# A larger ring, streamed values and a finer schedule in a decode kernel that reads a key-value cache

## The chip, the cores and the metric

One core of one Trainium2 chip. The metric is device time in microseconds (us) of one execution. Every run named here was at a granted TensorE clock of 1.00. A run reads some 2 us longer than the span of its profile.

## The reference, cut to what matters

One token per row, eight rows. Two layers, each attention plus a feed-forward, both with the same weights and the same cache:

```python
x = x + attention(layernorm(x), k_cache, v_cache, wq, wo)   # 32 heads of 128, 4096 keys
x = x + relu(layernorm(x) @ w1) @ w2                         # 640 -> 1728 -> 640
x = x + attention(layernorm(x), k_cache, v_cache, wq, wo)   # the same cache again
x = x + relu(layernorm(x) @ w1) @ w2
```

In bf16 the cache is 8 x 32 x 4096 x 128 x 2 x 2 bytes = 537 MB, far more than the on-chip memory, and it is needed twice: 1074 MB, less what is still on the chip at the second reading. The weights are 15 MB.

## The kernel before

A *visit* is one row, one layer and one pair of heads. A *dip* is a stretch of lower transfer rate; there is one at every row's end. It needs 4 units of keys and 4 of values, each 512 KB (128 partitions x 4 KB). All units pass through one ring, the *arena*; TensorE frees a unit once it has read it, and only then can the next load into it be issued. Some units of a row (`keep`) stay until its second layer has used them. The order of all work is fixed on the host by `plan`:

```python
UNIT, G, SPARE, SMALL, AHEAD = 4, 22, 6, 4, 3      # units per visit half, units of ring, ...
    keep = set()                                   # G - SPARE = 16 units stay for layer 1
    ...
            roomy = G - len(kept)                  # how many units one load brings
            n = 4 if keeping or roomy >= 16 else 2 if roomy >= SMALL else 1
    ...
            visits += nxt[:AHEAD] + cur + nxt[AHEAD:]   # AHEAD visits of the next row, then layer 1
```

Between the units of a visit `step()` mixes in one piece of each waiting chain: softmax, output projection, and at a row's end the feed-forward (`up` and `down`, 70 matmuls each, in one piece) and 160 query matmuls in four pieces. The values, per visit 64 pairs of weight load and one-column matmul:

```python
    nc.tensor.matmul(oy[i][:, h : h + 1], lhsT=arena[:, value block], rhs=P_tiles[i][:, h, j : j + 1], ...)
```

## Time and profile before

| what | before |
|---|---|
| time, median of 4 runs | 2524.51 us (2523.44 to 2529.79) |
| bytes moved by all DMA queues | 1027.07 MB |
| TensorE busy | 55% |

### The profile page before, as it was taken

To read this page: it belongs to the slowest core of one execution; us is meant where nothing else is said; L and a number is where in the kernel's file an instruction comes from. 1 tells how busy PE (TensorE), PEld (TensorE's weight loads), DVE (VectorE), ACT (ScalarE), POOL (GpSimd) and SP (SyncE) were. 2 spreads that over 40 slices of the span, in tenths; PEclk is the share of its full clock that TensorE was granted. 3 is DMA by queue.
4 is the path that set the end of the run, shared out by engine and by line. 5 is a ranking of instruction groups with operands and counts; after the bars stand their busy time and mean duration, and the time that the engine had idled before them with its cause. 6 is when DMAs were issued, how large, how long until landed. Compare 5 with 4: busy or idle time off the path is not lost.

```text
span 2521.7 us, 84569 instructions
## 1 busy us (share of the span) xinstructions
PE 1384.2 (55%) x40134; PEld 1299.3 (52%) x40134; DVE 320.4 (13%) x1707; ACT 288.2 (11%) x1422; POOL 0.7 (0%) x6
## 2 busy tenths in 40 slices
PE   3447545475454754557455574545645466445745
PEld 3336545464454744546454564545645455444744
DVE  0001111111111111111111111111111111111111
ACT  1001001010010100101010110101101011001200
POOL 0000000000000000000000000000000000000000
DMA  9999999999999999999999999999999999999897
GB/s 408 424 426 377 419 425 426 423 345 426 425 425 422 360 426 425 425 406 372 425 426 425 400 386 426 425 426 386 403 425 425 426 375 413 426 425 404 324 427 305
DMA packets 82525, 1027.07 MB, mean 407 GB/s; under 512 B 9220, under 2 KB 9220, under 8 KB 9220
## 3 DMA queue, kind: packets, MB, share of 16 engines
q1 hardware_dynamic: 82180, 1021.68, 97.4%
q8 instruction: 313, 5.13, 0.8%
q14 instruction: 32, 0.26, 0.0%
HBM read 1021.63 MB, written 0.01 MB: 405 GB/s over the span
## 4 chain that ended last, share of the span: by engine, by line
DMA 76%; PE 19%; issue 3%; ACT 1%; SPq 0%; DVE 0%; ACTq 0%
DMA arena<-in_A_k_cache_dram 38%; DMA arena<-in_A_v_cache_dram 37%; PE s_ps L397 6%; PE oy_ps L399 6%; PE blk_ps L434 1%; PE q_ps L371 1%; DMA wq_sb<-in_A_wq_dram 1%; PE oy_ps L449 1%; PE ch_ps L321 1%; PE ch_ps L338 1%; PE blk_ps L410 1%; ACT L428 0%; PE blk_ps L419 0%; PE ch_ps L300 0%; ACT P_sb L428 0%
## 5 line engine op out<-in xcount | busy, mean ns | idle before, releaser
L397 PE MATMUL s_ps<-q,arena 128*128 128x1 bf16 x16384 | 517.8, 165 | 586.7 <-DMA arena<-in_A_k_cache_dram 535.7
L399 PE MATMUL oy_ps<-P_sb,arena 128*128 128x1 bf16 x16384 | 519.6, 166 | 509.8 <-DMA arena<-in_A_v_cache_dram 482.6
L397 PEld LDWEIGHTS <-arena 128*128 128x128 bf16 x16384 | 479.5, 104 | 608.2 <-DMA arena<-in_A_k_cache_dram 553.8
L399 PEld LDWEIGHTS <-arena 128*128 128x128 bf16 x16384 | 481.5, 105 | 555.6 <-DMA arena<-in_A_v_cache_dram 500.2
L423 ACT ACTIVATE nmax<-blk_ps 128x2 f32<-128x2 f32 x256 | 44.1, 172 | 1987.5 <-PE blk_ps L419 1987.5
L438 DVE RECIPROCAL invL<-blk_ps 128x2 f32<-128x2 f32 x256 | 43.8, 171 | 965.2 <-PE blk_ps L434 965.2
L414 DVE TENSOR_REDUCE hmx<-blk_ps 2x1 f32<-2x128 f32 x256 | 71.3, 279 | 734.5 <-PE blk_ps L410 734.5
L434 PE MATMUL blk_ps<-lrow,ones_c 128*128 128x2 f32 x512 | 145.2, 353 | 1.9 <-issue 1.9
L428 ACT ACTIVATE P_sb<-s_ps,nmax 128x32 bf16<-128x32 f32 x512 | 142.4, 283 | 7.8
L449 PEld LDWEIGHTS <-wo_sb 128*128 128x128 bf16 x2560 | 131.7, 121 | 9.5 <-issue 9.3
L434 PEld LDWEIGHTS blk_ps<-lrow,ones_c 128*128 128x128 f32 x512 | 128.7, 311 | 3.5 <-issue 2.0
L449 PE MATMUL oy_ps<-oT,wo_sb 128*128 128x1 bf16 x2560 | 104.9, 165 | 8.7 <-issue 8.4
L428 ACT ACTIVATION_READ_ACCUMULATOR P_sb<-s_ps,nmax 128x1 f32 x512 | 100.2, 196 | 0.0
L406 DVE TENSOR_REDUCE mrow<-s_ps 128x2 bf16<-128x64 f32 x256 | 57.5, 225 | 213.9 <-PE s_ps L397 213.9
L410 PE MATMUL blk_ps<-ident,mrow 128*2 128x128 bf16 x256 | 68.3, 267 | 4.4 <-issue 4.2
L442 DVE TENSOR_TENSOR oT<-oy_ps,invL 128x2 bf16<-128x2 f32 x256 | 40.8, 160 | 159.4 <-PE oy_ps L399 159.4
L371 PEld LDWEIGHTS <-wq_sb 128*128 128x128 bf16 x1440 | 43.2, 105 | 11.2 <-issue 7.9
L338 PEld LDWEIGHTS <-w_sb 128*128 128x128 bf16 x1120 | 45.3, 107 | 6.4 <-issue 4.4
L338 PE MATMUL ch_ps<-hT,w_sb 128*128 128x1 bf16 x1120 | 45.8, 168 | 4.0 <-issue 3.7
L456 DVE TENSOR_TENSOR xT<-xT,oy_ps 128x5 f32<-128x5 f32 x256 | 41.0, 160 | 46.4 <-PE oy_ps L449 25.2
L419 PE MATMUL blk_ps<-diag,onesb_c 2*128 2x2 bf16 x256 | 46.8, 183 | 0.0
L371 PE MATMUL q_ps<-xq,wq_sb 128*128 128x1 bf16 x1280 | 40.0, 165 | 7.4 <-issue 7.4
(42 smaller groups left out, 324.4 us busy)
## 6 DMA issues: line engine op xcount, KB each, us to landing
arena<-in_A_v_cache_dram SPq DMA_DIRECT2D x208, 2048.0 KB, 21.9
arena<-in_A_k_cache_dram SPq DMA_DIRECT2D x192, 2048.0 KB, 22.4
arena<-in_A_k_cache_dram SPq DMA_DIRECT2D x96, 1024.0 KB, 8.6
arena<-in_A_v_cache_dram SPq DMA_DIRECT2D x64, 1024.0 KB, 7.2
wq_sb<-in_A_wq_dram SPq DMA_DIRECT2D x4, 1280.0 KB, 25.0
wo_sb<-in_A_wo_dram SPq DMA_DIRECT2D x4, 1280.0 KB, 34.3
w_sb<-in_B_w_dram SPq DMA_DIRECT2D x1, 2240.0 KB, 36.6
w_sb<-in_B_w_dram SPq DMA_DIRECT2D x1, 2160.0 KB
```

What stands on the lines that cost most here:

```text
L338: nc.tensor.matmul(y_ps[:, c : c + 1], lhsT=w2_sb[:fs, f, c * P : (c + 1) * P], rhs=st[key, "hT"][:fs, f : f + 1], start=(f == 0), stop=(f ...
L371: nc.tensor.matmul(q_ps[:, h, :], lhsT=wq_sb[:, g, c, h * Dh : (h + 1) * Dh], rhs=xl[:, c : c + 1] if layer else xl[:, :, c], start=(c == ...
L397: nc.tensor.matmul(s_tiles[i][:, h, j : j + 1], lhsT=lhsT, rhs=q, start=True, stop=True)
L399: nc.tensor.matmul(oy[i][:, h : h + 1], lhsT=lhsT, rhs=P_tiles[i][:, h, j : j + 1], start=(j == 0), stop=(j == NJ - 1),)
L406: nc.vector.tensor_reduce(out=m_tiles[i], in_=s_tiles[i], axis=AX.X, op=ALU.max)
L410: nc.tensor.matmul(blk[i][:2, :P], lhsT=m_tiles.pop(i), rhs=ident, start=True, stop=True)
L414: nc.vector.tensor_reduce(out=hmx, in_=blk[i][:2, :P], axis=AX.X, op=ALU.max)
L419: nc.tensor.matmul(blk[i][:, P : P + 2], lhsT=ones_b, rhs=nmax.pop(i), start=True, stop=True)
L423: nc.scalar.activation(out=nm, in_=blk[i][:, P : P + 2], func=ACT.Copy, scale=-inv_sqrt_dh)
L428: nc.scalar.activation(out=P_tiles[i][:, h, :], in_=S[:, h, :], func=ACT.Exp, bias=nm[:, h : h + 1], scale=inv_sqrt_dh, accum_out=l_tiles[ ...
L434: nc.tensor.matmul(blk[i][:, P + 2 : P + 4], lhsT=ones_f, rhs=l_tiles.pop(i), start=True, stop=True)
L449: nc.tensor.matmul(oy[i][:, 2 + c : 3 + c], lhsT=wo_sb[:, 2 * hp + h, c * P : (c + 1) * P], rhs=o[:, h : h + 1], start=(h == 0), stop=(h = ...
```

## The change

The intent: read less, by keeping more of the cache; and let TensorE hold up the loads less in the stretch where the ring is squeezed. The core of the diff:

```diff
-G = 22      SPARE = 6    SMALL = 4    AHEAD = 3
+G = 26      SPARE = 6    SMALL = 7    AHEAD = 4    CAP = 20
     def step():
-        for c in chains:                       # one piece of every chain
+        n = 0                                  # cheapest first, at most CAP matmuls in one step
+        for c in sorted(chains, key=lambda c: c[0][0]):
+            if not n or n + c[0][0] <= CAP:
+                n += c[0][0]
+                take(c)
     # feed-forward and queries
-    up: 70 matmuls, down: 70 matmuls, queries: 4 pieces of 40
+    up: 5 pieces of up to 15, down: 5 pieces of 14, queries: 16 pieces of 10
     # values: the probabilities are the weights, the values stream
-    matmul(oy[:, h:h+1], lhsT=arena[value block], rhs=P_tiles[:, h, j:j+1])            # 64 per visit
+    matmul(o_ps[32*c : 32*c+CJ, :], lhsT=P_tiles[:, h, j:j+CJ], rhs=arena[512 columns],
+           tile_position=(0, 32*c))                                                     # 16 per visit
+    nc.scalar.copy(out=o_tiles, in_=o_ps)                                               # then 4 gathering matmuls
     # sum of the softmax: one bf16 matmul and a reduction instead of ACT's accumulator and an fp32 matmul
     # layer 1: output projection, norm and feed-forward once for all 8 rows at the end, not row by row
     # square root of the per-row norms: 12 VectorE instructions instead of ScalarE's Sqrt
-    nc = Bacc("TRN2", ...)
+    nc = Bacc("TRN2", ..., dynamic_dma_scratch_size=32)      # memory for the larger ring
     # (cuts marked by comments; the layout of V in memory changes with the value matmul)
```

## The prediction

> **What bounds the kernel now.** I read the page first (busy shares, the forty slices, the queues, the chain of waits), then the timeline in stretches of 20 us over the whole span, then the chain of waits and the groups by line inside one slow stretch.
>
> ```profile
> span 2521.7 us, 84569 instructions
> PE 1384.2 (55%) x40134; PEld 1299.3 (52%) x40134; DVE 320.4 (13%) x1707; ACT 288.2 (11%) x1422; POOL 0.7 (0%) x6
> ...
> GB/s 408 424 426 377 419 425 426 423 345 426 425 425 422 360 426 425 425 406 372 425 426 425 400 386 426 425 426 386 403 425 425 426 375 413 426 425 404 324 427 305
> DMA packets 82525, 1027.07 MB, mean 407 GB/s; under 512 B 9220, under 2 KB 9220, under 8 KB 9220
> ...
> q8 instruction: 313, 5.13, 0.8%
> ...
> DMA 76%; PE 19%; issue 3%; ACT 1%; SPq 0%; DVE 0%; ACTq 0%
> ```
>
> No compute engine is busy for more than 55% of the span, and DMA is 76% of the chain. The GB/s row shows a ceiling near 425, left only in eight short dips (once per batch row) and at the end. So the time is bytes over 425 GB/s, plus what the dips, head and tail lose. The stretches of 20 us show both states; columns are PE, weight load, DVE, ACT, POOL, PE clock, DMA share, GB/s.
>
> ```profile
> 440.00:460.00 20.00, 10.07 (x305) 9.45 (x303) 2.28 (x12) 1.64 (x10) 0.00 (x0) 1.00 1.01 425
> ...
> 500.00:520.00 20.00, 11.35 (x322) 10.48 (x319) 3.22 (x19) 2.92 (x11) 0.00 (x0) 1.00 0.88 341
> 520.00:540.00 20.00, 16.20 (x442) 15.49 (x443) 3.44 (x20) 6.30 (x18) 0.00 (x0) 1.00 0.95 335
> 540.00:560.00 20.00, 14.26 (x444) 13.45 (x442) 2.51 (x14) 2.14 (x13) 0.00 (x0) 1.00 0.97 367
> ...
> 2500.00:2520.00 20.00, 11.73 (x297) 10.83 (x297) 2.66 (x15) 2.60 (x9) 0.00 (x0) 1.00 0.20 84
> ```
>
> The 98 stretches at 415 GB/s or more average 425.2. For each of the others I take 20 x (1 - GB/s / 425.2): the first loses 2.7 us, the last 16.0, the eight dips 85.6 (8.1, 11.8, 9.7, 10.7, 9.4, 9.0, 8.8, 17.9). Check: 1027.07 MB / 425.2 GB/s = 2415.5, plus 104.3 = 2519.8, against a span of 2521.7. This balance carries the prediction.
>
> What a dip is: the second row of its chain of waits.
>
> ```profile
> 516.65 7.43 DMA arena<-in_A_v_cache_dram
> 524.13 1.01 PE oy_ps L399 x32
> 525.25 2.18 PE ch_ps L321 x70
> 527.43 0.95 PE s_ps L397 x32
> ...
> 528.81 2.67 PE ch_ps L338 x70
> ...
> 540.64 1.37 issue
> ```
>
> From 524 to 563 us the chain is nearly all PE and its "issue" gaps (1.4, 1.6, 2.2 us): the row's feed-forward in lumps of 70 matmuls, the 160 query matmuls, and visits whose keys and values are already resident, which cost PE time but no DMA. Before that (505 to 524) PE waits for 1 MB loads. The cause is the same: 16 of the ring's 22 units of 512 KB hold data for layer 1, so six feed the stream, in pieces of two units, and a unit is refilled only after PE has read it.
>
> **What the Trainium skill says.** "HBM Reference", section Access, gives about 425 GB/s for a core that streams alone, bounded by its 16 DMA engines; the 425.2 above agrees, so I treat it as a ceiling no schedule will lift. "DMA: Bandwidth & Descriptors", section Bandwidth, measured 341 GB/s for one 1 MB transfer alone and 425 for 16 MB. The dips' 335 to 367 resemble the first, but inside the same dip, when several 1 MB loads are queued, 406 to 439 appear in 2.5 us stretches: depth counts too. "SBUF — State Buffer", section SBUF size, gives 224 KiB per partition less 16 KiB of DMA scratch. Weights take 114.4 KiB and 22 units 88 KiB, 202.4 of 208; 26 units need 218.4, which is why the change cuts the scratch to 32 bytes. "TensorE: Matmul & The Clock Gate" (Back-to-back issue gap; Part 3) puts a warm 512-column matmul at N/2.4 + 2.5 ns, about 216 ns, and three concurrent column tiles at 2.38 times one. No instruction of this trace shows either; the clock column is 1.00 throughout.
>
> **The change, part by part.** I counted loads in the kernel's own static plan.
>
> Bytes. The ring grows to 26 units, 20 kept instead of 16, so each of 8 rows saves four more units: K/V traffic falls from 1006.6 to 989.9 MB, 16.8 MB or 39.5 us at 425.2. This is on the path: DMA is the bound.
>
> Instructions. PE's list shrinks from 79,352 rows to 52,866, so of 84.6 thousand instructions about 26 thousand go; 5.13 MB of fetch falls by about 1.6 MB, 3.7 us, and the issue gaps should be rarer.
>
> PE. Values: before, 64 matmuls and weight loads per visit (a 32-matmul half takes 1.01 us, so 2.0). After, the four columns of probabilities are stationary and the values stream, 16 matmuls of 512 columns in four column groups. Estimate from the skill: 16 x 216 ns = 3.45 us in series, 1.4 overlapped by 2.4. The softmax sum loses its two fp32 passes (0.56 us to about 0.2). The output projection (0.41 us) goes in seven of eight layer-1 rows, and seven layer-1 feed-forwards go (5 us each), done at the end for all rows at once. Added: four gathering matmuls, 0.15 us. In the steady state PE has half its time free, so none of this is on the path. In the dip it is: 2.0 + 1.4 + some 1.0 of small work per visit against 4.8 before.
>
> ACT and DVE. ACT gains one 100 x 512 copy per visit (estimate 0.56 us, from 165 ns at 2 columns and 213 at 64) and loses two accumulator reads (0.39) and its square-root table switches (two of 1.28 us each time); DVE gains about 12 instructions of 0.16 us per norm. Neither is over 20% busy; hidden.
>
> Schedule. Feed-forward and query work is cut into pieces of at most 15 matmuls (0.5 us) between units, has four visits to finish instead of three, and the squeezed ring loads single units: per row 30 loads of 512 KB and 9 of 1 MB, instead of 20 of 1 MB. A freed unit is refilled at once, so five or six stay queued. Per squeezed visit DMA needs eight units, 9.9 us; PE about 3.4 for attention, 1 small and 2.4 of feed-forward, 6.8: it no longer binds. Only the five resident halves with 160 query matmuls (5.3 us) come near.
>
> Sum: 1027.07 - 16.8 - 1.6 = 1008.7 MB / 425.2 = 2372. Head and tail unchanged in kind: 19 (the last feed-forward still follows the last load). Dips: per row 15.7 MB of singles at an assumed 395 instead of 425 GB/s costs 2.8 us, 9.4 MB of pairs at 405 another 1.1, the resident stretch 0.5: 4.4 x 8 = 35. The 395 and 405 are my choice between the dip's 345 and the ceiling. Span 2426; runs read 1.7 us above the span: 2428, which is 3.8% less.
>
> **The rivals.**
> Dips stay, in a new form: 512 KB loads run at the old dip's 345 GB/s. 15.7 MB then loses 8.6 us per row, 69 in all: 2372 + 19 + 69 = 2460, still 2.5% faster. For it: the fixed cost of a transfer and a ring that is again six units. Against: more of it is in flight.
> Column groups do not overlap: V costs 3.45 us per visit. Steady state is unmoved (10 of 20 us busy becomes 13), but dips become PE-bound again, 85 us plus up to 40: about 2515, no change. Against: the array is divided by column strips and the four outputs lie in different ones.
> Dips vanish: 2372 + 19 + 5 = about 2396, 5.1% faster.
> Worse than before: it would need a stall in every visit, for instance on the single-buffered value accumulator, which the copy must empty before the next visit. A whole K visit lies between; I give it little.
>
> **Range and chances.** Low 2398 is the floor with closed dips; high 2468 the first rival with a little more. The 2% line is at 2474: only the second rival, or dips as large as before plus extra tail, is beyond it. Faster 0.88, within 2% 0.11, slower 0.01.
>
> **What would show it.** Read bytes near 1005 MB plus fetch near 3.5; the steady 425 unchanged; the eight dips as shallower slices, 380 to 415; PE's busy share down or its count near 27 thousand; V's matmuls spaced about 60 to 100 ns, not 216; no lump of 70 feed-forward matmuls on the chain; 512 KB loads landing in some 7 us. I am wrong if dips stay at 340, if V's matmuls hold PE for over 3 us per visit, or if a wait appears in the steady stretches.

## The result, and the profile after

| | before | after |
|---|---|---|
| median time | 2523.69 us (13 runs, 2519.12 to 2529.79) | 2403.58 us (8 runs, 2402.26 to 2406.83) |
| ratio | | 0.9525, 95% interval 0.9516 to 0.9535 |

A ratio is the mean time of one kernel's fast runs over that of the other's of the same rounds, so not quite the ratio of the medians. The later medians of the kernel before (2523.5 to 2525.7) come from the rounds of each group of experiments.

The page of the changed kernel (span, first part, then from the second, third and fourth part):

```profile
span 2400.5 us, 57552 instructions
PE 1278.0 (53%) x26486; PEld 790.7 (33%) x26486; DVE 380.9 (16%) x1984; ACT 338.4 (14%) x1179; POOL 0.7 (0%) x6
...
GB/s 407 429 430 411 428 430 430 429 402 430 429 430 428 402 430 430 428 428 407 428 430 430 415 412 429 430 431 411 420 429 430 429 404 424 430 430 418 416 429 292
DMA packets 100854, 1008.59 MB, mean 420 GB/s; under 512 B 11268, under 2 KB 11268, under 8 KB 41988
...
q8 instruction: 207, 3.39, 0.5%
...
DMA 82%; PE 15%; DVE 2%; issue 1%; ACT 1%; SPq 0%; ACTq 0%
```

The bytes are the predicted ones (1008.7). The dips are shallow. And the plateaus read 428 to 430 where they read 425 to 426: that was not foreseen. The same stretches of 20 us as before (columns as there), one undisturbed, the second dip, and the last:

```profile
440.00:460.00 20.00, 9.28 (x194) 5.55 (x194) 2.73 (x14) 2.45 (x8) 0.00 (x0) 1.00 1.01 429
480.00:500.00 20.00, 11.13 (x256) 7.39 (x256) 3.07 (x17) 2.45 (x8) 0.00 (x0) 1.00 0.94 394
500.00:520.00 20.00, 16.11 (x323) 11.69 (x321) 5.52 (x32) 2.68 (x10) 0.00 (x0) 1.00 1.01 395
520.00:540.00 20.00, 18.12 (x417) 12.77 (x416) 6.05 (x34) 5.06 (x27) 0.00 (x0) 1.00 1.02 418
540.00:560.00 20.00, 15.54 (x334) 9.47 (x331) 4.41 (x22) 4.44 (x14) 0.00 (x0) 1.00 1.02 430
...
2380.00:2400.00 20.00, 11.45 (x203) 7.61 (x199) 3.13 (x16) 3.67 (x9) 0.00 (x0) 1.00 0.08 32
```

TensorE is busier in the dip than it was (18 of 20 us), yet DMA keeps 395 to 430 GB/s. The balance, made as in the prediction (mean of all 20 us stretches at 415 GB/s or more as the undisturbed rate; the loss of each other stretch from it):

| us unless noted | MB | undisturbed GB/s | MB over rate | eight dips | head, tail, rest |
|---|---|---|---|---|---|
| before, span 2521.7 | 1027.07 | 425.2 | 2415.7 | 85.4 | 20.6 |
| after, span 2400.5 | 1008.59 | 428.4 | 2354.1 | 25.0 | 21.4 |

The 121.2 us of the span divide into 43.5 for fewer bytes (18.48 MB at 425.2), 18.2 for the higher rate (1008.59 MB at 425.2 against 428.4), 60.4 for the dips, and -0.8 for the ends. (The prediction says 98 undisturbed stretches and 85.6 us of dips; a recount gives 97 and 85.4.)

### The profile page after: what moved, and what is told of

Its sections match the earlier page's. It is cut to its first block, busy times and chain, and to the rows that moved or that the text cites.

```text
span 2400.5 us, 57552 instructions
## 1 busy us (share of the span) xinstructions
PE 1278.0 (53%) x26486; PEld 790.7 (33%) x26486; DVE 380.9 (16%) x1984; ACT 338.4 (14%) x1179; POOL 0.7 (0%) x6
## 2 busy tenths in 40 slices
DMA packets 100854, 1008.59 MB, mean 420 GB/s; under 512 B 11268, under 2 KB 11268, under 8 KB 41988
## 4 chain that ended last, share of the span: by engine, by line
DMA 82%; PE 15%; DVE 2%; issue 1%; ACT 1%; SPq 0%; ACTq 0%
DMA arena<-in_A_k_cache_dram 68%; DMA arena<-in_A_v_cache_dram 14%; PE s_ps L452 7%; PE o_ps L440 4%; PE q_ps L424 2%; ACT o_sb L498 1%; PE oy_ps L503 1%; PE oy_ps L520 1%; DVE hmx L466 0%; DVE root L341 0%; PE blk_ps L471 0%; PE blk_ps L462 0%; DVE diag L468 0%; PE ch_ps L316 0%; DVE root L343 0%
## 5 line engine op out<-in xcount | busy, mean ns | idle before, releaser
L440 PE MATMUL o_ps<-arena,P_sb 128*4 128x512 bf16 x4096 | 557.2, 606 | 563.0 <-DMA arena<-in_A_v_cache_dram 559.2
L452 PEld LDWEIGHTS <-arena 128*128 128x128 bf16 x16384 | 493.1, 104 | 523.6 <-DMA arena<-in_A_k_cache_dram 515.9
L440 PEld LDWEIGHTS <-P_sb 128*4 128x4 bf16 x4096 | 105.7, 83 | 666.7 <-issue 657.9
L466 DVE TENSOR_REDUCE hmx<-blk_ps 2x1 f32<-2x128 f32 x256 | 71.3, 278 | 676.3 <-PE blk_ps L462 676.3
L498 ACT CAST o_sb<-o_ps 100x512 bf16<-100x512 f32 x256 | 150.1, 586 | 104.5 <-PE o_ps L440 104.5
L490 DVE TENSOR_REDUCE lsum<-blk_ps 128x2 f32<-128x64 f32 x256 | 57.5, 225 | 398.3 <-PE blk_ps L484 398.3
L471 PEld LDWEIGHTS <-onesb_c 2*128 2x128 bf16 x256 | 25.1, 98 | 135.4 <-issue 135.4
L503 PE MATMUL oy_ps<-gsel,o_sb 100*128 100x2 bf16 x1024 | 63.8, 166 | 4.7 <-ACT o_sb L498 0.7
L513 DVE TENSOR_TENSOR oT<-oy_ps,invL 128x2 bf16<-128x2 f32 x128 | 20.4, 159 | 275.2 <-PE oy_ps L503 275.2
L513 DVE TENSOR_TENSOR o<-oy_ps,invL 128x2 bf16<-128x2 f32 x128 | 21.4, 167 | 268.1 <-PE oy_ps L503 268.1
L484 PE MATMUL blk_ps<-P_sb,onesb_c 128*128 128x64 bf16 x256 | 60.0, 234 | 1.1 <-ACT P_sb L479 1.1
L520 PE MATMUL oy_ps<-oT,wo_sb 128*128 128x1 bf16 x1280 | 51.8, 165 | 0.0
L520 PEld LDWEIGHTS <-wo_sb 128*128 128x128 bf16 x1440 | 50.9, 105 | 0.8 <-issue 0.8
L503 PEld LDWEIGHTS <-o_sb 100*128 100x128 bf16 x1024 | 47.4, 105 | 9.0 <-ACT o_sb L498 8.0
```

The costliest lines, as they stand in the source:

```text
L440: nc.tensor.matmul(o_ps[32 * c : 32 * c + CJ, :], lhsT=P_tiles[i][:, h, j : j + CJ], rhs=arena[:, at + c * CJ * Dh : at + (c + 1) * CJ * D ...
L452: nc.tensor.matmul(s_tiles[i][:, j : j + 1], lhsT=arena[:, at + n * P : at + (n + 1) * P], rhs=q, start=True, stop=True)
L466: nc.vector.tensor_reduce(out=hmx, in_=blk[i][:2, :P], axis=AX.X, op=ALU.max)
L471: nc.tensor.matmul(blk[i][:, P : P + 2], lhsT=ones_b, rhs=nmax.pop(i), start=True, stop=True)
L484: nc.tensor.matmul(blk[i][:, P + 2 :], lhsT=ones_p, rhs=P_tiles[i].rearrange("p h j -> p (h j)"), start=True, stop=True)
L490: nc.vector.tensor_reduce(out=L, in_=blk.pop(i)[:, P + 2 :].rearrange("p (h j) -> p h j", h=2), axis=AX.X, op=ALU.add)
```

## The experiments

Twelve kernels, all with correct results. The same balance for each; "rest" as above.

| run | median us | ratio to before | undisturbed GB/s | dips us | rest us |
|---|---|---|---|---|---|
| changed kernel | 2403.58 | 0.9525 | 428.4 | 25.0 | 21.4 |
| e1_ring22 | 2441.30 | 0.9668 | 428.5 | 25.1 | 21.6 |
| e2_old_ring26 | 2488.75 | 0.9855 | 424.3 | 85.8 | 20.4 |
| e3_more_instr | 2460.98 | 0.9748 | 428.1 | 74.4 | 23.5 |
| e4_old_values | 2433.86 | 0.9641 | 428.0 | 50.4 | 19.8 |
| e5_off64 | 2424.37 | 0.9597 | 426.0 | 32.6 | 22.5 |
| e6_old_aligned | 2505.79 | 0.9923 | 428.2 | 79.7 | 19.7 |
| e7_pairs | 2434.60 | 0.9636 | 429.2 | 60.4 | 22.0 |
| e8_lumps | 2447.70 | 0.9692 | 428.8 | 72.8 | 21.7 |
| e9_sqrt | 2407.81 | 0.9541 | 428.6 | 30.6 | 22.4 |
| e10_spare5 | 2423.01 | 0.9598 | 428.9 | 60.1 | 21.6 |
| e11_spare4 | 2471.48 | 0.9791 | 429.0 | 111.2 | 22.4 |
| e12_ahead3 | 2447.16 | 0.9696 | 429.0 | 71.3 | 22.4 |

### Where does the higher rate come from?

Three theories at first: the deeper ring (depth), fewer instructions to fetch (fetch), values streamed through TensorE instead of loaded as its weights (value path).

**e1_ring22**: the changed kernel with the old ring.

```diff
-G = 26
+G = 22
```

> The changed kernel with the old ring of 22 units (16 kept, still six free when squeezed). All theories: 16.8 MB more is read, 39 us at 428 GB/s. Theory depth (the undisturbed stretches rose from 425.2 to 428.4 GB/s because six instead of five 2 MB loads are queued): the undisturbed rate falls back to 425 and costs 18 us more, about 2461 us. Theories fetch (fewer instructions to fetch) and value path (values stream through TensorE instead of being loaded as weights): the rate stays at 428 to 430, about 2443 us. Dips as in the changed kernel, about 25 us in all, in every theory that puts them down to schedule and load size.

Measured 2441.3 us, undisturbed rate 428.5, dips 25.1. Depth falls; the 37.7 us are the bytes. The size of the ring has no part in closing the dips, as long as six units stay free.

**e2_old_ring26**: the kernel before with the new ring.

```diff
-G = 22
+G = 26
-nc = Bacc("TRN2", ...)
+nc = Bacc("TRN2", ..., dynamic_dma_scratch_size=32)
```

> The kernel before with the ring of 26 units, 20 kept, and the DMA scratch cut to 32 bytes; nothing else. All theories: 16.8 MB less, 39.5 us. Theory depth: undisturbed rate rises to 428, 18 us more, about 2466 us. Fetch and value path: rate stays at 425, about 2484 us. The dips keep their 85 us if they come from the lumps and the pair loads; if a larger kept set were what closed them, they would shrink to some 30 and the time would be near 2430.

Measured 2488.75 us: 36.3 us less than the 2525.06 of its rounds, the bytes again; rate 424.3, dips 85.8. Depth falls a second time, from the other side.

**e3_more_instr**: 11 idle matmuls after each value unit.

```diff
+            for n in range(11):
+                nc.tensor.matmul(idle_ps, lhsT=arena[:, at + n * P : at + (n + 1) * P],
+                                 rhs=P_tiles[i][:, 0, n : n + 1], start=True, stop=True)
```

> The changed kernel plus 44 idle one-column matmuls with their weight loads per visit (22.5 thousand instructions, 1.4 MB of fetch, 1.4 us of TensorE time per visit), result unused. Theory fetch: the undisturbed rate falls from 428 to about 425 or 426, 14 to 18 us, plus 3.4 us for the fetched bytes, plus up to 15 us in the dips: 2420 to 2440 us. Depth and value path: the undisturbed rate stays at 428, only the 3.4 us and the dips' part: 2407 to 2422 us. If column-group overlap and a lighter TensorE were what closed the dips, they should come back here by more than 15 us.

Measured 2460.98 us: the rate stays at 428.1, so fetch falls as the cause of the rate. But the dips go from 25.0 to 74.4, far above the 15 us foreseen. TensorE time in the squeezed stretch is dear: the idle matmuls take 1.5 us per visit (TensorE is busy for 1669.0 us against 1278.0) and bring most of the old loss back.

**e4_old_values**: the old value matmul and V layout, in the new schedule.

```diff
-            16 matmuls of 512 columns into o_ps, a copy, 4 gathering matmuls
+            nc.tensor.matmul(oy[i][:, h : h + 1], lhsT=arena[:, at + n * P : at + (n + 1) * P],
+                             rhs=P_tiles[i][:, h, j : j + 1], ...)
```

> The changed kernel with the values computed in the old way (value blocks as weights, 64 one-column matmuls per visit, no gathering, no copy on ScalarE) and the old layout of V; all else of the change stays. About the same number of added instructions as the run with idle matmuls. Theory value path: undisturbed rate back to 425, 18 us, about 2425 us; theory fetch: the same fall here and in the run with idle matmuls; theory depth: rate stays at 428 and the time within 5 us of 2404. My view that the value path itself bought little in the dips: dips within 10 us of the changed kernel's 25 us. The rival that streaming the values is what freed TensorE: dips grow by 30 us or more, 2435 us and above.

Measured 2433.86 us: rate 428.0, so the value path is not the cause of the rate either. The dips grow by 25 us, between the two views; mine, that the value path bought little, was wrong.

All three theories had fallen. What was left had to be common to every variant of the changed kernel and absent from the kernel before and e2. The intervals between the moments at which TensorE gets its next 2 MB load show that each load itself is shorter in the changed kernel. From the timeline of TensorE (start, duration, what; in brackets what it waited for), the kernel before and then the changed one:

```profile
641.30 1.01 PE L399 MATMUL oy_ps<-P_sb,arena 128*128 128x1 bf16 x32 [2.34 <-DMA arena<-in_A_v_cache_dram]
646.19 1.01 PE L397 MATMUL s_ps<-q,arena 128*128 128x1 bf16 x32 [2.63 <-DMA arena<-in_A_k_cache_dram]
651.08 1.01 PE L399 MATMUL oy_ps<-P_sb,arena 128*128 128x1 bf16 x32 [2.33 <-DMA arena<-in_A_v_cache_dram]
```

```profile
630.55 0.60 PE L440 MATMUL o_ps<-arena,P_sb 128*4 128x512 bf16 x4 [2.87 <-DMA arena<-in_A_v_cache_dram]
635.40 0.59 PE L452 MATMUL s_ps<-q,arena 128*128 128x1 bf16 x16 [2.33 <-DMA arena<-in_A_k_cache_dram]
640.23 0.60 PE L440 MATMUL o_ps<-arena,P_sb 128*4 128x512 bf16 x4 [2.85 <-DMA arena<-in_A_v_cache_dram]
```

4.89 us per load before (646.19 - 641.30), 4.83 to 4.85 after. Over whole traces the middle value is 4.84 to 4.85 in the changed kernel, e1, e3 and e4, and 4.90 to 4.91 before and in e2. The compiled programs differ in one thing more, which no theory had named and no profile shows: where the ring starts in a partition. It is address 134848 before (192 bytes past a multiple of 256), 118496 in e2 (224 past), and 119040, a multiple of 256, in the changed kernel and all variants of it so far: the new constants and the smaller scratch had shifted it. So a fourth theory: the start address.

**e5_off64** and **e6_old_aligned**: the same 64 bytes put ahead of the ring, in the changed kernel and in the kernel before.

```diff
+    kv.tile([P, 32], BF16, name="pad")
     arena = kv.tile([P, G * GW], BF16, name="arena")
```

> The changed kernel with one edit: a 64-byte tile ahead of the ring, so that its first byte moves from address 119040 (a multiple of 256) to 119104. New theory start address: the per-load time of 4.84 us for 2 MB in all kernels whose ring starts at a multiple of 256, against 4.89 in the two whose ring starts at 192 or 224 past one, comes from that. It expects the undisturbed loads at 4.89 us, the undisturbed rate near 425 GB/s and 15 to 20 us more, about 2421 us. The rival, that something else of the new schedule raised the rate: no difference, within 4 us of 2404.

> The kernel before with the same 64-byte tile ahead of its ring, which moves the start from 134848 (192 past a multiple of 256) to 134912 (a multiple of 256). Start address: undisturbed loads 4.84 us, undisturbed rate 428 to 429 GB/s, 14 to 20 us less than before, about 2507 us. Rival: unchanged, within 5 us of before.

Measured: e5 2424.37 us, 20.8 more than the changed kernel; e6 2505.79 us, 19.9 less than the 2525.66 of its rounds (ratio 0.9923, interval 0.9905 to 0.9941). The timeline of e5:

```profile
626.58 0.60 PE L441 MATMUL o_ps<-arena,P_sb 128*4 128x512 bf16 x4 [2.91 <-DMA arena<-in_A_v_cache_dram]
631.47 0.58 PE L453 MATMUL s_ps<-q,arena 128*128 128x1 bf16 x16 [2.37 <-DMA arena<-in_A_k_cache_dram]
636.36 0.60 PE L441 MATMUL o_ps<-arena,P_sb 128*4 128x512 bf16 x4 [2.92 <-DMA arena<-in_A_v_cache_dram]
```

4.89 us again, from one pad. The timeline of e6:

```profile
645.70 1.01 PE L400 MATMUL oy_ps<-P_sb,arena 128*128 128x1 bf16 x32 [2.29 <-DMA arena<-in_A_v_cache_dram]
650.54 1.01 PE L398 MATMUL s_ps<-q,arena 128*128 128x1 bf16 x32 [2.57 <-DMA arena<-in_A_k_cache_dram]
655.38 1.01 PE L400 MATMUL oy_ps<-P_sb,arena 128*128 128x1 bf16 x32 [2.28 <-DMA arena<-in_A_v_cache_dram]
```

4.84 us; over the whole trace mostly 4.84 to 4.86. The start address is shown as the cause of the shorter loads, in both directions. The pad moves only the ring and the small working tiles behind it, which take no part in these loads. By the balance the longer loads are 13.4 us of what e5 lost, and its dips grew by 7.6 more; e6 gained 16.9 by the rate and 5.7 in the dips (its profiled run was the fastest of six). Not shown is which alignment it takes: the slow starts, 64, 192 and 224 bytes past a multiple of 256, are no multiples of 128 either. The Trainium skill, "DMA: Bandwidth & Descriptors", section How a descriptor splits into AXI transactions, says that a transaction must start at a multiple of 256 bytes and that a descriptor which does not start there costs extra beats. Its example is a read; here the memory side was the same and the on-chip side moved. That the same splitting acts on the written side fits, but is argued, not shown.

### What closed the dips?

**e7_pairs**: the squeezed ring loads two units at a time again.

```diff
-SMALL = 7
+SMALL = 4
```

> The changed kernel with the squeezed ring loading pairs (1 MB) again instead of single units. Load size theory: a pair is refilled only when both its units have been read, so fewer bytes are queued; dips grow from 25 us by 15 to 40, about 2430 us. Rival, that only the order and amount of TensorE work set the dips: within 6 us of 2404.

Measured 2434.6 us, dips 60.4: 35 more. Load size theory holds.

**e8_lumps**: `up` and `down` as one piece each (counted as one matmul, so that `CAP` lets them in).

```diff
-    up_parts = [range(f, min(f + 3, FC)) for f in range(0, FC, 3)]      # and DC pieces of down
+    up_parts = [range(FC)]                                              # and one piece of down
```

> The changed kernel with each feed-forward layer as one lump of 70 matmuls again instead of five pieces of 14 or 15; queries stay cut. Lump theory: TensorE holds back the refill for 2.3 and 2.8 us twice per row, dips grow by 10 to 25 us, about 2420 us. Rival, that six queued units cover such a pause (7.4 us of transfer): within 5 us of 2404.

Measured 2447.7 us, dips 72.8: 48 more, twice what I had expected. The chain of waits in its second dip (start, length, what) shows why:

```profile
508.09 0.57 PE ch_ps L316 x2
509.31 0.23 DVE root L341
...
511.33 2.22 PE ch_ps L357 x70
513.66 0.53 PE o_ps L441 x4
514.19 2.77 PE ch_ps L375 x70
```

From the start of the norm's second matmul (508.1) to the end of `down` (517.0) are 8.9 us. In these the timeline of TensorE has three value units read (the chain shows one of them), where the transfers could have brought seven (512 KB at 428 GB/s are 1.22 us): TensorE waits 0.9 us for VectorE's square root ahead of `up`, and the two lumps take 5.0 us. I had counted the lumps alone.

**e12_ahead3**: three visits of the next row ahead of the second layer.

```diff
-AHEAD = 4
+AHEAD = 3
```

> The changed kernel with three visits of the next row ahead of a row's second layer instead of four. Slack theory (the fourth visit is needed so that the cut feed-forward, norms and queries are done before the first resident visit): TensorE has to run the rest of that chain in one go, dips grow from 25 by 10 to 25 us, about 2420 us. Rival: three visits are enough for pieces this small, and one squeezed visit fewer per row makes the dips smaller; 2390 to 2400 us, a kernel faster than the changed one.

Measured 2447.16 us, dips 71.3: 46 more. The queries of the first resident visit are now needed before the cut chain is through. From the waits of TensorE in 490 to 570 us (waited for: us, times, longest) and the stretch it falls in:

```profile
PE q_ps L424 <- DVE xq L326: 2.7, 1, 2.7
```

```profile
520.00:540.00 20.00, 14.72 (x365) 11.69 (x362) 5.09 (x29) 4.05 (x20) 0.00 (x0) 1.00 0.77 293
```

Slack theory holds, at about twice the size expected (10 to 25 us): TensorE waits for the last norm of the chain, and DMA falls to 293 GB/s.

**e9_sqrt**: the square root on ScalarE again.

```diff
-            if nb == 1:
-                inverse_root(rstd, st[key, "var"])
+            (always) nc.scalar.activation(out=std, in_=st[key, "var"], func=ACT.Sqrt, ...); reciprocal
```

> The changed kernel with the square root of the per-row norms on ScalarE again (one activation and a reciprocal, with a table switch before and after) instead of the 12 VectorE instructions. Root theory: those 12 instructions (2.4 us in order on VectorE, twice per row) delay the next visit's maximum and hold TensorE, a new wait that the change put into the dips; without them up to 10 us less, about 2395 us. Rival, that they were worth their place: the two table loads of 1.28 us stand in front of the exponentials and the value step, dips grow by 5 to 20 us, about 2415 us.

Measured 2407.81 us (ratio 0.9541, interval 0.9526 to 0.9555; the changed kernel 0.9525), dips 30.6. The root theory misses: without the VectorE root the kernel is no faster. Its rival has the direction and, with 5.6 us of dips, its lower edge, but not the 2415 us. In the changed kernel TensorE waits behind the root:

```profile
PE blk_ps L471 <- DVE diag L468: 10.0, 8, 1.4
```

Eight waits of up to 1.4 us, one per dip. In e9 they are gone, but TensorE waits eight times for ScalarE's copies of the queries instead (7.6 us, longest 1.0). So e9 compares two ways to the root; what the waits themselves cost is not shown.

**e10_spare5** and **e11_spare4**: keep 21 or 22 units, leave five or four free.

```diff
-SPARE = 6
+SPARE = 5      # e11: 4
```

> The changed kernel keeping 21 units of 26, five free when squeezed. Bytes: 4.2 MB less, 9.8 us. If five queued units (6.1 us of transfer) still cover what TensorE holds back, about 2394 us. If six is the edge, dips grow by 10 us or more and it is 2404 or above.

> The changed kernel keeping 22 units of 26, four free when squeezed. Bytes: 8.4 MB less, 19.6 us. If four units cover the pauses, 2384 us. I expect they do not (4.9 us of transfer against waits of 4 to 5 us on resident loads[...]): dips from 25 to 60 us or more, 2420 us or above.

Measured 2423.01 and 2471.48 us: the bytes fell as reckoned (to 1004.40 and 1000.20 MB), but the dips rose from 25.0 to 60.1 and 111.2. Six is the edge: each unit of ring given to the kept set saves 9.8 us of traffic and costs 35, then 51 us of dips. No variant beats the changed kernel.

### Why do the old values cost 25 us in the dips?

Not by TensorE's busy time. Groups by line for the values, before and after (x count, busy us, mean ns of one, then idle time ahead):

```profile
L399 PE MATMUL oy_ps<-P_sb,arena 128*128 128x1 bf16 x16384 | 519.6, 166 | 509.8 <-DMA arena<-in_A_v_cache_dram 482.6
```

```profile
L440 PE MATMUL o_ps<-arena,P_sb 128*4 128x512 bf16 x4096 | 557.2, 606 | 563.0 <-DMA arena<-in_A_v_cache_dram 559.2
```

Over 256 visits that is 2.03 us per visit before and 2.18 after. Both figures count each group to the modelled end of its last matmul. How far the new matmuls overlap is read from their starts. Two fours in a row, each with one matmul per column group:

```profile
485.12 0.59 PE L440 MATMUL o_ps<-arena,P_sb 128*4 128x512 bf16 x4 [2.78 <-DMA arena<-in_A_v_cache_dram]
...
485.50 0.74 PE L440 MATMUL o_ps<-arena,P_sb 128*4 128x512 bf16 x4
```

They start 0.38 us apart, some 95 ns per matmul or 1.5 us per visit. The formula of the Trainium skill, "TensorE: Matmul & The Clock Gate", section Back-to-back issue gap, gives 216 ns for one alone, so the overlap is an estimated 2.3; no run here times one alone. What changed more are the gaps in which TensorE waits for nothing the profile shows. From the waits of TensorE: before, changed, e4 (old values) and e3 (idle matmuls, as many instructions as e4):

```profile
PE s_ps L397 <- issue: 41.7, 29, 2.7
PE oy_ps L399 <- issue: 27.1, 19, 2.6
```

```profile
PE s_ps L452 <- issue: 4.6, 8, 1.6
```

```profile
PE oy_ps L441 <- issue: 41.2, 23, 2.4
PE s_ps L452 <- issue: 40.8, 26, 2.6
```

```profile
PE s_ps L458 <- issue: 8.3, 15, 1.3
```

Summed over all lines, the gaps are 98.1 us before, 9.9 after, 100.7 in e4 and 21.1 in e3. They lie in the dips, on the chain (13.5% of it in e4's stretch from 780 to 860 us), in pieces of 0.8 to 2.4 us. e3 and e4 have 80,080 and 79,822 instructions, so the count alone does not make the gaps. The transfer records of the traces show what ends them: of the gaps of 0.8 us or more, all 53 before, all 53 in e4, all 4 after and all 9 in e3 end 1.2 to 1.6 us after a transfer of the instruction queue (q8, 16 KB each) has landed. These come some 8 us apart (313 in 2522 us before), so by chance only one gap in twenty or so would end there: in these gaps TensorE waits for instructions. That long runs of one-column matmuls (1.01 us for 32, some 32 ns each) use them up faster than they come fits e3 and e4, and that the gaps are what cost e4 its 25 us fits too; no run took the gaps away alone, so both are argued.

## Why the prediction was right, and where it was off

- **Time**: 2403.58 us, in the range of 2398 to 2468 and 24 us below the middle. The direction, faster by over 2%, was right, as were the balance as a method and DMA as the bound. That it came so close to the low end is in part luck: against the predicted span the rate gave 18 us that nobody had foreseen, the dips 10, and the ends took 2 back.
- **Bytes**: right to 0.1 MB (1008.7 against 1008.59); e1 and e2 show that the ring buys this alone, 36 to 38 us.
- **Rate**: wrong. "I treat it as a ceiling no schedule will lift" is the step that failed. The schedule did not lift it, the address did: each load went from 4.89 to 4.84 us, 18.2 us of the balance; e5 and e6 moved the time by 20 to 21 us, 13 to 17 of it by the rate. (The skill's 425 GB/s stands in the section Specifications (TRN2) of "HBM Reference".)
- **Dips**: the mechanism right, the size off. 35 us expected, 25.0 measured, from 85.4. The term that was mis-sized is that of the singles "at an assumed 395 instead of 425 GB/s": the squeezed stretches from 505 to 525 us run at 405 to 421 and lose 0.7 us. Of this dip's 3.2 us 2.1 lie in a hole just before, at 497.5 to 505, which the sum does not have.
- **"PE no longer binds"**: half right. In 520 to 540 us TensorE is busy for 18.1 of 20 us and on the chain; it binds there, but without pauses long enough to empty the queue. The slack is thin: e3 spends 1.5 us more per visit and loses 49 us in the dips.
- **Value matmuls**: 1.4 us expected per visit, from an overlap of 2.4; by their starts they take 1.5, an overlap of 2.3, so right. They freed little all the same (busy time 2.03 before, 2.18 after). Why the dips grow by 25 us without them (e4) is argued: the vanished issue gaps fit, which the prediction had named only as "rarer".
- **VectorE and ScalarE "hidden"**: not quite. One wait of TensorE for VectorE of up to 1.4 us per dip is new. Its cost is not shown; e9 has only that ScalarE's root costs 4 us more.
- **Ends**: 19 expected, 21.4 measured. Rival one (singles at 345 GB/s) and rival two (no overlap) did not come. The third, closed dips, has a span of 2396 against the measured 2400.5, but by luck: it has 5 us of dips where 25.0 are left, and the unforeseen rate makes up for them.

The single parts do not add up: undone alone, pieces bring back 48 us of dips, the fourth visit 46, single loads 35, the value path 25. Together that is more than the 60 that all of them won. A dip stays closed only while TensorE, its pauses included, frees units about as fast as they land, so each of these four is needed, and none has a share of its own. Not undone alone by any run, and so without a measured part, are the work of layer 1 moved to the end (seven feed-forwards and output projections fewer between the rows), the sum of the softmax and `CAP`. What still loses 25 us is partly seen: at 497.5 to 505 us DMA falls to 239, 346 and 342 GB/s, after TensorE has waited 4.75 us for a kept value load of 2 MB, whose reading frees nothing. TensorE's wait of 1.45 us for VectorE ends at 505.1, in the same hole. No run separated the two, or tested a smaller piece there.

## What to carry to other kernels

In a kernel that is bound by transfers, write its time as bytes over the undisturbed rate plus what each dip loses, and compare two kernels term by term; a term that moves without a reason given for it, as the rate did here, is a finding. A squeezed ring does not need a faster engine so much as one whose longest pause between two refills is shorter than the time that the queued loads last: cut lumps, load in the unit that is freed, and leave the chain slack. And look at the address at which a large buffer starts before taking a measured rate for a ceiling.

## What the Trainium skill lacked or had wrong

- "DMA: Bandwidth & Descriptors", section How a descriptor splits into AXI transactions, gives the cost of a descriptor that does not start at a multiple of 256 bytes, with a read as its example. It lacks the on-chip side: a ring that starts 64, 192 or 224 bytes past such a multiple took 4.89 to 4.91 us per 2 MB load against 4.84 to 4.85, about 1%; the pad changed the time of the two kernels by 20 to 21 us.
- "DMA: Bandwidth & Descriptors", section Bandwidth, sets 1 MiB as the size for 75% of peak. It lacks the part of the queue: loads of 512 KB, issued some 7 us before they landed (the time of five or six of them), ran at 405 to 421 GB/s here.
- "TensorE: Matmul & The Clock Gate", Part 3, has 2.38 for three column tiles and no figure for four. Four column groups of 4 weight columns and 512 moving ones started 0.38 us after the four before them here, an estimated 2.3 by the page's figure for one alone.
- "Runtime: NRT & Kernel Launch", section Instruction fetch mechanics, says that going on to the next block of 16 KiB of instructions is mostly hidden. In the dips here it is not: TensorE's gaps sum to 98.1 us in the kernel before and 100.7 in e4_old_values, and each of 0.8 us or more ends 1.2 to 1.6 us after such a block has landed. With 512-column value matmuls 9.9 us are left.
